# Hedgehog attention and a layer-normed MLP on one core: MLP groups of 512 tokens in place of 384, and every pair of batches worked off in units of two heads of one batch

## The chip, the cores and the metric

One core of a Trainium2 chip runs the whole program. The metric is the device time of one execution in microseconds (us): the kernel before takes 380.07 us, the median of 3 runs (379.72 to 380.33). "PE" is the matrix engine (TensorE), "PEld" its weight loads, "DVE" the vector engine, "ACT" the scalar engine, "POOL" GpSimd and "SP" the engine that issues nearly all transfers.

## What is computed

The inputs are q, k, v of shape 8 batches x 8 heads x 576 tokens x 64, a feature matrix 64 x 128, and the MLP's gain and two weight matrices (512 x 2048 and 2048 x 512).

```
def phi(x):
    proj = np.einsum('bhsd,df->bhsf', x, w_phi)
    proj = proj - np.max(np.abs(proj), axis=-1, keepdims=True)
    return np.concatenate([np.exp(proj), np.exp(-proj)], axis=-1)
q_p, k_p = (phi(q), phi(k))
kv = np.einsum('bhsf,bhsd->bhfd', k_p, v)
z = np.sum(k_p, axis=2)
num = np.einsum('bhsf,bhfd->bhsd', q_p, kv)
den = np.einsum('bhsf,bhf->bhs', q_p, z)[..., None] + 1e-06
...
# x: the 8 heads of num / den side by side, 8 x 576 x 512
xn = (x - mu) / np.sqrt(var + 1e-06) * g_ln
ch = np.maximum(xn @ w_ch1, 0.0) @ w_ch2
return (x + ch).astype(np.float32)
```

## The kernel before

**Tiles.** The 8 batches go in four pairs. The 576 tokens of a batch are 4 tiles of 128 and a rest of 64; the two rests of a pair make one "mixed" tile (MX = 8), so that a pair has NT = 9 tiles of 128 tokens, and the program 36.

**Attention** runs in 32 units, 8 to a pair, and a unit is two head-sequences. In pair 0 a unit is two heads of one batch: units 0 to 3 finish batch 0, units 4 to 7 batch 1. In pairs 1 to 3 a unit is one head of both batches, so that a batch is complete only when all 8 units of its pair are. PE turns or takes turned q and k (`qkT`), multiplies by the features (`pm` for k and q, `pt` for q the other way round, `n_bank` or `px` for the mixed tile), DVE takes the maxima (`m`, line 889), ACT the exponentials (`eb` line 903, `ea` line 971), POOL scales v (`vv`, line 915), PE multiplies features and values (`n_bank`, lines 997 and 1003) and then `num` (lines 1074 and 1080, in two parts), DVE joins and inverts (`numc`, `rden`, lines 1098 to 1110), and POOL writes the quotient into the bf16 `x` of the pair ("put", line 1118). In pair 0 half of the mixed rows lie on the wrong partitions: they go to `xs` and are moved by a transfer (line 1028) once per batch.

**The MLP** runs in 12 groups of RN = 384 tokens (three tiles), three groups to a pair. Of each tile the mean and variance are taken (`st`, `mv`), it is centred (`xc`) and turned, by PE in pair 0 (`xT_ps`) and by DMA transposes after. Then come 16 blocks of 4 matmuls 128x384 (`hT_ps`, line 1339), each evicted through a ReLU by ACT or DVE (lines 1349, 1347), and per tile 16 matmuls 128x512 (`ch_ps`, line 1406), whose result is scaled, joined with x and stored. Groups 0 to 2 are cut through the tiles in order: group 0 has tiles 0 to 2 of batch 0, so that it waits for units 0 to 3; groups 1 and 2 wait for all 8 units. In a later pair all three groups wait for the pair's last unit.

**Order of the work.** A planner written in the kernel (class `Order`) is run when the program is built. It is given every operation with an engine, a duration, what it reads and writes and which of the PSUM banks (A: 2 for `pm` and `pt`, N: 1, B: 3 for `hT_ps`, `ch_ps` and, in pair 0, `num`) it takes and frees. It picks for each engine the ready operation of the lowest rank; ranks are latest-start times plus offsets from the table `OFF`, by stage and by unit. The MLP's due times come from `DUE` and `BLOCK`. The result is one fixed instruction list for each engine. Where PE would idle before 75 us the planner puts in "fillers", small matmuls on zeros (line 1607), which keep PE occupied and compute nothing. PE waits in the order of its list: what stands behind a waiting instruction waits too.

Of the kernel before, what the change touches and what calls it, by code (L numbers as in the profile page):

```python
# [17 lines left out]
def bcast(ap: bass.AP, dim: int, n: int) -> bass.AP:  # L18
# [6 lines left out]
BLOCK = 17.68  # L25
# [8 lines left out]
FOLD = 0  # L34
# [4 lines left out]
        "load": 291.2, "trans": -8.3, "trans.copy": 32.9, "mixed": 7.1, "mixed.max": 32.9,  # L39
        "mixed.exp": 102.3, "mixed.fold": 0.0, "k": 28.8, "k.max": -2.5, "k.em": -28.4,  # L40
        "k.exp": -35.8, "en": 34.8, "vv": 1.8, "q": -0.7, "q.max": -15.1, "q.em": -14.1,
        "tails": -11.4, "tails.exp": -31.1, "kv": -2.9, "kv.copy": -20.8, "num0": -58.7,
        "num1": 49.3, "num.dve": -42.9, "g1": 0.0, "g2": 0.0, "g3": 0.0, "put": 7.3,
# [3 lines left out]
        "load": 291.2, "trans": -47.2, "trans.copy": 36.5, "mixed": 3.9, "mixed.max": 11.9,  # L47
        "mixed.exp": 12.0, "mixed.fold": 0.0, "k": 40.0, "k.max": -21.4, "k.em": 23.2,
        "k.exp": 42.8, "en": -19.5, "vv": 39.6, "q": -16.4, "q.max": 21.9, "q.em": -3.0,
        "tails": -100.2, "tails.exp": -42.9, "kv": 200.0, "kv.copy": -9.7, "num0": 87.9,  # L50
        "num1": 81.6, "num.dve": -5.2, "g1": 0.0, "g2": 0.0, "g3": 0.0, "put": -19.2, "ln": 5.4,
        "w1": -144.2, "w2": -136.8, "ln.c": -23.8, "ln.t": -23.8,
    },
    {
        "load": 291.2, "trans": 33.0, "trans.copy": 240.4, "mixed": -15.3, "mixed.max": -17.9,
        "mixed.exp": 83.6, "mixed.fold": 0.0, "k": 37.2, "k.max": -11.0, "k.em": -3.3,
        "k.exp": 18.4, "en": -32.8, "vv": 12.0, "q": 304.0, "q.max": -11.2, "q.em": -3.1,
        "tails": 103.2, "tails.exp": -35.5, "kv": 7.2, "kv.copy": 27.1, "num0": 39.1,
        "num1": 98.0, "num.dve": 2.1, "g1": 0.0, "g2": 0.0, "g3": 0.0, "put": -66.5,
        "ln": -23.8, "w1": -144.2, "w2": 26.3, "ln.c": -23.8, "ln.t": -23.8,  # L60
    },
    {
        "load": 291.2, "trans": 230.9, "trans.copy": 78.9, "mixed": 191.2, "mixed.max": -32.0,
        "mixed.exp": 33.8, "mixed.fold": 0.0, "k": -8.1, "k.max": 2.2, "k.em": -87.4,
        "k.exp": 26.7, "en": 11.2, "vv": -77.6, "q": -9.4, "q.max": 38.5, "q.em": -38.3,
        "tails": 16.8, "tails.exp": 26.2, "kv": 13.6, "kv.copy": 16.6, "num0": -1.3,
        "num1": 43.6, "num.dve": 21.7, "g1": 0.0, "g2": 0.0, "g3": 0.0, "put": 5.4, "ln": 14.4,
        "w1": -144.2, "w2": -136.8, "ln.c": 117.0, "ln.t": -36.8,
    },
    {  # L70
        "load": 14.8, "trans": -15.4, "trans.copy": -27.6, "mixed": 131.2, "mixed.max": -9.9,
        "mixed.exp": 10.9, "mixed.fold": 0.0, "k": -79.5, "k.max": -17.0, "k.em": 19.9,
        "k.exp": 31.1, "en": -13.2, "vv": -36.7, "q": 271.6, "q.max": 5.6, "q.em": 13.9,
        "tails": -412.8, "tails.exp": -3.4, "kv": 97.7, "kv.copy": 26.5, "num0": -27.8,
        "num1": -4.0, "num.dve": 68.7, "g1": 29.8, "g2": -16.9, "g3": -5.0, "put": -27.1,
# [3 lines left out]
        "load": 6.3, "trans": 29.0, "trans.copy": 24.9, "mixed": -2.7, "mixed.max": -13.2,  # L79
        "mixed.exp": -3.8, "mixed.fold": 0.0, "k": -79.5, "k.max": 30.5, "k.em": -14.6,  # L80
        "k.exp": -25.7, "en": -17.2, "vv": -13.4, "q": 271.6, "q.max": 28.1, "q.em": 39.7,
        "tails": -412.8, "tails.exp": 34.3, "kv": 2.4, "kv.copy": 35.9, "num0": 26.5,
        "num1": 69.2, "num.dve": 40.9, "g1": -233.9, "g2": -41.7, "g3": 25.5, "put": -6.4,
        "ln": 112.0, "w1": -341.2, "w2": -67.5, "ln.c": 107.2, "ln.t": 107.2,
    },
    {
        "load": 25.7, "trans": 38.5, "trans.copy": -37.8, "mixed": 31.6, "mixed.max": 60.6,
        "mixed.exp": 9.0, "mixed.fold": 0.0, "k": -79.5, "k.max": 11.5, "k.em": 44.1,
        "k.exp": 303.5, "en": 21.2, "vv": -17.8, "q": 271.6, "q.max": -32.9, "q.em": -6.4,
        "tails": -412.8, "tails.exp": -14.4, "kv": -2.0, "kv.copy": 123.1, "num0": 24.3,  # L90
        "num1": -4.7, "num.dve": 32.8, "g1": 92.8, "g2": 69.4, "g3": -5.0, "put": -14.8,
# [3 lines left out]
        "load": 6.3, "trans": 104.7, "trans.copy": -63.0, "mixed": -16.2, "mixed.max": -21.2,  # L95
        "mixed.exp": -28.3, "mixed.fold": 0.0, "k": -79.5, "k.max": -12.7, "k.em": -22.0,
        "k.exp": 14.6, "en": 103.8, "vv": 290.4, "q": 271.6, "q.max": -41.3, "q.em": 39.4,
        "tails": -412.8, "tails.exp": 4.2, "kv": -18.4, "kv.copy": -14.2, "num0": -20.5,
        "num1": 307.7, "num.dve": -20.9, "g1": -233.9, "g2": -41.7, "g3": 52.2, "put": 25.6,
        "ln": 131.6, "w1": -341.2, "w2": -67.5, "ln.c": 241.5, "ln.t": 47.3,  # L100
    },
    {
        "load": 276.1, "trans": 161.1, "trans.copy": 96.2, "mixed": -19.1, "mixed.max": -57.1,
        "mixed.exp": 54.1, "mixed.fold": 0.0, "k": -33.5, "k.max": 27.3, "k.em": 127.3,
        "k.exp": 30.4, "en": 12.5, "vv": 20.5, "q": -27.3, "q.max": 25.9, "q.em": 283.8,
        "tails": -210.6, "tails.exp": 11.0, "kv": 17.1, "kv.copy": -31.1, "num0": 152.9,
        "num1": 148.0, "num.dve": -174.3, "g1": 25.2, "g2": 33.5, "g3": -17.3, "put": -21.0,
        "ln": 196.2, "w1": -0.3, "w2": 28.2, "ln.c": 104.9, "ln.t": 37.2,
    },
    {  # L110
        "load": 4.0, "trans": 3.2, "trans.copy": 96.2, "mixed": -24.7, "mixed.max": -26.5,
        "mixed.exp": -33.8, "mixed.fold": 0.0, "k": -33.5, "k.max": 16.7, "k.em": -34.1,
        "k.exp": -3.4, "en": -54.3, "vv": 37.4, "q": -27.3, "q.max": 12.5, "q.em": 28.4,
        "tails": -210.6, "tails.exp": -22.6, "kv": 46.6, "kv.copy": -25.9, "num0": 16.8,
        "num1": 66.4, "num.dve": -83.9, "g1": 5.0, "g2": -21.1, "g3": -12.8, "put": -8.3,
        "ln": 20.8, "w1": 193.2, "w2": 28.2, "ln.c": 31.7, "ln.t": 4.8,
# [193 lines left out]
def kernel(  # L310
# [33 lines left out]
    RN = 384  # L344
    NR = ST // RN
    NM = RN // P
# [70 lines left out]
    for i in range(2):  # L417
# [5 lines left out]
    nident = consts.tile([P, P], BF16, name="nident")  # L423
    nc.vector.tensor_scalar(
        out=nident, in0=ident, scalar1=minus, scalar2=None, op0=ALU.mult
    )
# [4 lines left out]
    xs = consts.tile([P, 4, D], BF16, name="xs")  # L431

# [7 lines left out]
    ex_bufs = [consts.tile([P, 2, 2, P], BF16, name=f"ex{i}") for i in range(2)]  # L440
# [65 lines left out]
    def load_main(key, n, nu, rank, queue):  # L506
# [7 lines left out]
        if pair == 0:  # L514
# [5 lines left out]
            issue(  # L520
                queue, rank, dst.rearrange("p u (a f) -> p (u a) f", a=2), src,
                [(key + str(half), g % NBUF, u) for u in us for half in range(2)]
                + [("came", key, n)],
                262144 * nu,
            )
            return
# [212 lines left out]
    def a_mixed(u):  # L739
# [19 lines left out]
        def fold():  # L759
            subtract(u, u["px"][:, 2 * F : 3 * F], MX, u["mx"])  # L760

        def exps():
            ps = u["px"]
            for t, sc in ((0, 1.0), (1, -1.0)):
                if folded(n):
                    nc.scalar.activation(
                        u["EX"][:, t, :, :].rearrange("p s f -> p (s f)"), ps[:, F : 3 * F],
                        AF.Exp, scale=sc,
                    )
                    continue  # L770
# [195 lines left out]
    def a_tails(u):  # L966
# [680 lines left out]
```

## Time and profile before

| | |
|---|---|
| time | 380.07 us, median of 3 (379.72 to 380.33) |
| span of the profiled execution | 377.5 us, 2.57 us less than that median |
| PE busy | 363.6 us, 96% of the span, 3714 matmuls, 421 of them fillers |
| DVE, ACT, POOL busy | 250.5, 262.8, 203.4 us |
| DMA | 53.32 MB, mean 141 GB/s |

The profiled execution has no time of its own beside its span, so the 2.57 us (load, end of program) are taken as what lies around it. A matmul's recorded duration includes its way through the array; the pace of a run of equal matmuls is the time between starts. 128x384 goes at 0.1625 us and 128x512 at 0.2157 us. The profile of the program's second half shows PE alone at work with its evictions; the first 80 us show all engines busy and PE partly on fillers.

### The profile page before, as it was taken

The page shows a single profiled execution, that of the slowest core. Times are in us where ns is not written, and L with a number is a line of the kernel's source. Part 1 is how long each engine was busy: PE and PEld are TensorE (multiplying, and loading weights), DVE is VectorE, ACT ScalarE, POOL GpSimd, SP SyncE. Part 2 cuts the span into 40 slices and gives each one's busy share as a digit, 9 for nine tenths or more (in the row PEclk, how much of TensorE's full clock was granted, in tenths as well). Part 3 has the DMA queues.
Part 4 walks back from the last instruction along what each step waited for, and adds up shares of the span by engine and source line. Part 5 has one row for each costly group of instructions (what it writes and reads, how often), then busy time and mean ns, then how long its engine had stood idle before and what let it go on. Part 6 is the DMA issues. An engine that isn't in the chain of part 4 may idle for free.

```text
span 377.5 us, 9637 instructions
## 1 busy us (share of the span) xinstructions
PE 363.6 (96%) x3714; PEld 226.1 (60%) x3714; DVE 250.5 (66%) x548; ACT 262.8 (70%) x588; POOL 203.4 (54%) x347
## 2 busy tenths in 40 slices
PE   8998889799999999999999999999999999999995
PEld 8887766465656555665655555565565555555543
DVE  4788989997989879977877799587868200000001
ACT  2987978699697978896868778867846434444430
POOL 4399968659787754557857674635553001111121
PEclk9999999899999999999999999999999999999999
DMA  7999999899797867596826466500002520110012
GB/s 212 270 213 276 205 289 178 232 312 233 220 281 188 151 190 186 142 212 177 142 85 79 101 155 176 102 2 28 31 30 64 100 74 30 33 52 28 28 58 84
DMA packets 91086, 53.32 MB, mean 141 GB/s; under 512 B 57488, under 2 KB 86480, under 8 KB 91040
## 3 DMA queue, kind: packets, MB, share of 16 engines
q1 hardware_dynamic: 86000, 47.66, 52.1%
q0 software_dynamic: 4416, 4.49, 7.0%
q8 instruction: 29, 0.48, 0.5%
q10 hardware_dynamic: 624, 0.56, 0.5%
q14 instruction: 17, 0.14, 0.1%
HBM read 36.77 MB, written 9.44 MB: 122 GB/s over the span
## 4 chain that ended last, share of the span: by engine, by line
PE 79%; DVE 8%; DMA 6%; POOL 3%; ACT 1%; issue 1%; SPq 1%; ACTq 0%; DVEq 0%
PE hT_ps L1339 32%; PE ch_ps L1406 32%; DMA qk<-in_q_dram 4%; PE pm L827 3%; PE n_bank L1003 3%; DVE m L889 2%; PE num L1074 2%; DMA v<-in_v_dram 2%; PE pt L836 2%; PE n_bank L1074 1%; POOL vv L915 1%; PE n_bank L997 1%; PE ch_ps L1371 1%; DVE numc L1098 1%; DVE numc L1104 1%
## 5 line engine op out<-in xcount | busy, mean ns | idle before, releaser
L1339 PE MATMUL hT_ps<-xT,w 128*128 128x384 bf16 x768 | 153.2, 329 | 0.5 <-DVE numc L1098 0.3
L1406 PE MATMUL ch_ps<-w,hT 128*128 128x512 bf16 x560 | 148.1, 379 | 0.1
L1349 ACT ACTIVATE hT<-hT_ps 128x384 bf16<-128x384 f32 x125 | 61.6, 494 | 69.6 <-PE hT_ps L1339 69.2
L1339 PEld LDWEIGHTS <-w 128*128 128x128 bf16 x768 | 72.2, 99 | 56.7 <-issue 2.5
L889 DVE TENSOR_REDUCE m<-pm 128x8 f32<-128x1024 f32 x64 | 76.9, 1215 | 14.2 <-PE pm L827 12.2
L1406 PEld LDWEIGHTS <-hT 128*128 128x128 bf16 x560 | 51.1, 98 | 42.8 <-issue 1.2
L1118 POOL TENSOR_TENSOR x<-numc,rden 128x192 bf16<-128x192 f32 (+3 forms) x88 | 46.4, 541 | 47.3 <-DVE rden L1110 45.7
L903 ACT ACTIVATE eb<-pm 128x1024 bf16<-128x1024 f32 x64 | 64.7, 1038 | 7.6 <-DVE m L889 7.6
L971 ACT ACTIVATE ea<-pt 128x1024 bf16<-128x1024 f32 x64 | 63.7, 1039 | 5.1 <-PE pt L836 4.6
L1425 POOL TENSOR_TENSOR o<-o,x 128x512 f32<-128x512 f32 x20 | 23.1, 1156 | 80.3 <-ACT o L1419 80.3
L915 POOL TENSOR_TENSOR vv<-v,em 128x512 bf16<-128x512 f32 x32 | 34.0, 1064 | 34.4 <-issue 22.4
L1414 DVE SCALAR_TENSOR_TENSOR o<-ch_ps,rstd,x 128x512 f32<-128x512 f32 x15 | 11.2, 745 | 50.6 <-PE ch_ps L1406 50.6
L1347 DVE TENSOR_SCALAR hT<-hT_ps 128x384 bf16<-128x384 f32 x67 | 36.9, 553 | 11.6 <-PE hT_ps L1339 11.0
L915 POOL TENSOR_TENSOR vv<-v,en 128x512 bf16<-128x512 f32 x32 | 33.9, 1059 | 0.0
L1607 PE MATMUL n_bank<-wz 128*128 128x120 bf16 x421 | 30.7, 225 | 0.1
L1074 PEld LDWEIGHTS <-ea 128*128 128x128 bf16 x512 | 24.4, 97 | 8.1 <-issue 1.8
L1003 PE MATMUL n_bank<-vv,eb 128*128 128x65 bf16 x512 | 26.9, 194 | 0.0
L1607 PEld LDWEIGHTS <-wz 128*128 128x128 bf16 x421 | 26.0, 103 | 1.5 <-issue 0.5
L1003 PEld LDWEIGHTS <-eb 128*128 128x128 bf16 x512 | 22.3, 98 | 5.1 <-issue 1.5
L1261 DVE BATCH_NORM_STATS2 st<-x 128x6 f32<-128x512 bf16 (+1 forms) x44 | 24.6, 578 | 0.3 <-POOL x L1118 0.3
L1098 DVE TENSOR_TENSOR numc<-num,em 128x390 f32<-128x390 f32 (+1 forms) x40 | 20.6, 515 | 5.8 <-PE num L1074 5.5
L827 PE MATMUL pm<-wbk,qkT 64*128 64x128 bf16 x448 | 19.7, 217 | 2.8 <-ACT eb L903 2.8
(95 smaller groups left out, 456.8 us busy)
## 6 DMA issues: line engine op xcount, KB each, us to landing
qk<-in_k_dram SPq DMA_DIRECT2D x32, 256.0 KB, 4.9
qk<-in_q_dram SPq DMA_DIRECT2D x31, 256.0 KB, 5.5
v<-in_v_dram SPq DMA_DIRECT2D x31, 256.0 KB, 4.5
out_dram<-o SPq DMA_DIRECT2D x31, 256.0 KB, 2.5
w<-in_moe_w_ch_dram POOLq DMA_DIRECT2D x8, 512.0 KB, 11.5
out_dram<-o SPq DMA_DIRECT2D x10, 128.0 KB, 2.4
qx<-in_k_dram SPq DMA_DIRECT2D x16, 64.0 KB, 4.5
qx<-in_q_dram SPq DMA_DIRECT2D x14, 64.0 KB, 3.6
```

The lines of the kernel that those rows point to most:

```text
L889: nc.vector.reduce_max(out=m, in_=ps, axis=AX.X, apply_absolute_value=True)
L903: nc.scalar.activation(eb, ps, AF.Exp, scale=(1.0, -1.0)[t])
L915: nc.gpsimd.tensor_tensor(out=u["vv"][:, t, 0:MX, 0:D], in0=vb[:, hh, :].rearrange("p (c d) -> p c d", d=D), in1=bcast(e[:, 0:MX], 2, D), ...
L971: nc.scalar.activation(u["EA"][:, t, 0:1024], u["pt"], AF.Exp, scale=(1.0, -1.0)[t])
L1003: nc.tensor.matmul(ps[:, t, c // 4, :], EB[:, t, c, :], vv[:, t, c, :], start=False, stop=(t == 0 and c == MX - 1), skip_group_check=True,)
L1074: nc.tensor.matmul(ps[t][:, i, :], ea(u, t, c), KV[:, t, c // 4, :], start=True, stop=True,)
L1118: nc.gpsimd.tensor_tensor(out=dst, in0=st["numc"][ps_, i : i + n, 0:D], in1=bcast(st["rden"][ps_, i : i + n], 2, D), op=ALU.mult,)
L1339: nc.tensor.matmul(st["ps"], w1_sb[:, kc, jj * P : (jj + 1) * P], xT_bufs[(pair * NR + r) % XB][:, kc::KC, :], start=(kc == 0), stop=(kc = ...
L1347: nc.vector.tensor_relu(h_sb, st["ps"])
L1349: nc.scalar.activation(h_sb, st["ps"], AF.Relu)
L1406: nc.tensor.matmul(ch[t], hT[r, jj][:, rt * P : (rt + 1) * P], w2_sb[:, jj, :], start=(jj == 0), stop=(jj == JC - 1),)
L1607: nc.tensor.matmul(warm, wz, wz[:, 0:WN], start=False, stop=False, skip_group_check=True)
```

## The change

1. The MLP runs in nine groups of RN = 512 tokens (four tiles). Groups 2p and 2p+1 are the four full tiles of the two batches of pair p. The four mixed tiles of the program go to a tensor `xm` of their own and form one group, MIX, number 7; the second batch of pair 3 is group 8, LAST. 16 blocks of 4 matmuls 128x512 take the place of 128x384 ones.
2. All four pairs take pair 0's form: a unit is two heads of one batch (`BW = 4`). Group 2p then waits for the first four units of its pair, and group 2p+1 for the other four. Loads of pairs 1 to 3 become one transfer of 512 KB instead of two of 256 KB. Puts of these pairs go by head (3 tiles, 1 tile, 64 mixed rows), and the `xs` rows are moved once per batch in each pair: 8 moves instead of 2.
3. The `num` parts of pairs 1 to 3 take tiles (0,1,2,4,5,6) and (3,7,mixed) instead of 0 to 5 and 6 to 8; sizes are the same. `x` is tracked by tile, no longer by three.
4. The second product runs ahead of the first: a group's 64 `ch_ps` matmuls are offered within 10 of the next group's 16 blocks (`AHEAD_H`).
5. `hT` has 24 buffers of 512 instead of 34 of 384; unused code (`FOLD`, `nident`) goes. `BLOCK` and all of `OFF` have new numbers, so that every list is ordered anew.

```diff
-BLOCK = 17.68
+BLOCK = 23.57
...
-        "load": 291.2, "trans": -8.3, "trans.copy": 32.9, "mixed": 7.1, "mixed.max": 32.9,
+        "load": 291.2, "trans": -38.2, "trans.copy": 0.5, "mixed": 98.0, "mixed.max": 104.5,
...
-    RN = 384
-    NR = ST // RN
-    NM = RN // P
+    NM = 4
+    RN = NM * P
+    NR = MX // NM
+    LAST = NPAIR * NR
+    MIX = LAST - 1
+    HB = 24
+    AHEAD_H = 10
+    BW = 4
...
-        if pair == 0:
-            return i // 4, 2 * (i % 4) + half, 2
+        if pair < BW:
+            return 2 * pair + i // 4, 2 * (i % 4) + half, 2
...
-                out=u["x"][b * 64 : b * 64 + 64, MX, :].rearrange(
+                out=xm[b * 64 : b * 64 + 64, u["pair"], :].rearrange(
...
+    def token_tile(g, i):
+
+        pair, t = (i, MX) if g == MIX else (g // NR, g % NR * NM + i)
+        if g > MIX:
+            pair, t = NPAIR - 1, MX - NM + i
+        return pair, t, xm[:, i, :] if t == MX else pairs[pair]["x"][:, t, :]
...
+    def moe(g):
+
+
+        done = 0
+        for jj in range(JC):
+            if g <= LAST:
+                first(g, jj)
+            until = min(NM * JC, -(-(jj + 1) * NM * JC // AHEAD_H))
+            while g > 0 and done < until:
+                i, j0 = divmod(done, JC)
+                if g > LAST and i == NM - 1:
+                    break
+                n = min(until - done, JC - j0)
+                second(g - 1, i, j0, n)
+                done += n
...
-                half = i // 4 if i % 4 == 3 else None
...
+            if pair < BW:
+                groups = {3: (pair * NR,), 7: (pair * NR + 1,)}.get(i, ())
```

Counted over the whole lists, PE has 576 first-product matmuls of 128x512 where it had 768 of 128x384, 32 transposes of `xc` where it had 36, and 393 fillers after the first where it had 421; everything else on PE has the same count. POOL's puts rise from 96 instructions to 192. Of the 24 casts of q and k to bf16, DVE did 10, ACT 5 and POOL 9; now DVE does 3, ACT 14 and POOL 7.

**PE near unit 8**, the first unit of pair 1. `pm` and `pt` are its feature products, `n_bank<-wbk` the mixed tile's, `num` belongs to unit 7, `hT_ps` to group 0. Before:

```order
L1339 MATMUL hT_ps<-xT_139,w_134 128x384
...
L827 MATMUL pm<-wbk,qkT_142 128x128
...
L749 MATMUL n_bank<-wbk,qkT_142 128x256
...
L1074 MATMUL num<-KV,ea_127 128x65
...
L1080 MATMUL num<-KV,ea_127 128x65
...
L827 MATMUL pm<-wbk,qkT_143 128x128
...
L836 MATMUL pt<-qkT_143,wbk 128x512
...
L1339 MATMUL hT_ps<-xT_139,w_134 128x384
```

And in the changed kernel:

```order
L1019 MATMUL num<-KV,ea_127 128x65
...
L749 MATMUL n_bank<-wbk,qkT_141 128x256
...
L796 MATMUL pm<-wbk,qkT_141 128x128
...
L1246 MATMUL hT_ps<-xT_138,w_132 128x512
...
L749 MATMUL n_bank<-wbk,qkT_142 128x256
...
L1246 MATMUL hT_ps<-xT_138,w_132 128x512
...
L1013 MATMUL num<-KV,ea_127 128x65
...
L1246 MATMUL hT_ps<-xT_138,w_132 128x512
...
L796 MATMUL pm<-wbk,qkT_142 128x128
...
L805 MATMUL pt<-qkT_142,wbk 128x512
```

Between the two `pm` groups there stood both parts of `num`, one after the other, and no MLP matmul; now 16 `hT_ps` matmuls (8, 4 and 4) stand there, and the small part of `num` comes ahead of the first `pm` group.

**POOL in a unit of a later pair.** `vv<-...,em` and `vv<-...,en` scale v, the rows with `numc` are the puts. Before:

```order
L915 TENSOR_TENSOR vv<-v_101,em 128x8x64
...
L915 TENSOR_TENSOR vv<-v_101,en 128x8x64
...
L708 TENSOR_TENSOR b_1_147<-qk_100,one 128x1024
L1425 TENSOR_TENSOR o<-o,x 128x512
L1118 TENSOR_TENSOR x<-numc,rden 128x6x64
L1118 TENSOR_TENSOR x<-numc,rden 128x3x64
L915 TENSOR_TENSOR vv<-v_103,em 128x8x64
```

And in the changed kernel:

```order
L879 TENSOR_TENSOR vv<-v_101,em 128x8x64
...
L1057 TENSOR_TENSOR xm<-numc,rden 64x64
L879 TENSOR_TENSOR vv<-v_101,en 128x8x64
...
L1057 TENSOR_TENSOR xs<-numc,rden 64x64
L1057 TENSOR_TENSOR x<-numc,rden 128x64 x2
L1057 TENSOR_TENSOR x<-numc,rden 128x3x64 x2
L879 TENSOR_TENSOR vv<-v_101,em 128x8x64
```

Two puts per unit have become six, and some stand between or ahead of the scalings.

**SP at the end of attention** in the changed kernel (`xm<-xs` is the move of the mixed rows, `xT` are the transposes of groups 6, 8 and 7):

```order
L976 DMA xm<-xs 64x4x64
L1221 DMA out_dram<-o 128x512
L1161 DMA_TRANSPOSE xT_138<-xc_136 128x16x128
L1221 DMA out_dram<-o 128x512 x3
L976 DMA xm<-xs 64x4x64
L1161 DMA_TRANSPOSE xT_140<-xc_136 128x16x128
L1161 DMA_TRANSPOSE xT_139<-xc_137 128x16x128
L1221 DMA out_dram<-o 128x512 x4
```

Before, three transposes of 12 tiles for the last pair stood there, with no move ahead of them. On PE there stand behind the last `num` 16 `hT_ps` matmuls, 64 of `ch_ps` and 4 of `hT_ps` before the first that reads the MIX group's `xT_139`.

More of the change, by code (lines that the diff above doesn't have):

```diff
@@ L70 @@
-    {
[L71 to L75, printed above, removed]
+        "load": 291.2, "trans": 67.9, "trans.copy": 77.3, "mixed": 113.2, "mixed.max": 2.5,
@@ L110 @@
-    {
[L111 to L116, printed above, removed]
+        "load": 6.3, "trans": 1.6, "trans.copy": -2.9, "mixed": 203.3, "mixed.max": -49.1,
@@ L1050, in products @@
             KV = u["KV"]
[L1051 removed]
+            if part:
                 ps = n_bank if pair else ps_B.tile([P, 512], FP32, tag="B", name="num")
```

605 lines of the change are left out of this document (248 added, 357 removed), and 3 rows, old and new, of the table OFF.

## The prediction
> **What bounds the kernel now.** I read the page first, then the busy time by stage, then the chain of waits in order of time, and PE's own timeline where a stage had gaps. The page (part 2 has 40 slices of 9.4 us):
>
> ```profile
> span 377.5 us, 9637 instructions
> PE 363.6 (96%) x3714; PEld 226.1 (60%) x3714; DVE 250.5 (66%) x548; ACT 262.8 (70%) x588; POOL 203.4 (54%) x347
> PE   8998889799999999999999999999999999999995
> DVE  4788989997989879977877799587868200000001
> L1607 PE MATMUL n_bank<-wz 128*128 128x120 bf16 x421 | 30.7, 225 | 0.1
> ```
>
> PE is the bound, but its busy time holds 30.7 us of fillers, and the first eight slices have holes. Busy time by stage (columns: length, PE, PEld, DVE, ACT, POOL, granted clock, DMA share, GB/s):
>
> ```profile
> 40.00:60.00 20.00, 17.20 (x264) 13.12 (x262) 18.43 (x45) 17.66 (x40) 15.58 (x36) 1.00 1.23 249
> 60.00:80.00 20.00, 16.85 (x224) 11.43 (x223) 19.01 (x46) 15.84 (x34) 12.43 (x31) 0.91 0.90 224
> 80.00:100.00 20.00, 20.00 (x219) 11.81 (x218) 17.30 (x32) 17.71 (x40) 18.82 (x28) 1.00 1.01 238
> 100.00:180.00 80.00, 79.91 (x828) 47.31 (x825) 70.62 (x154) 66.78 (x158) 51.97 (x81) 1.00 0.81 197
> 180.00:260.00 80.00, 80.00 (x820) 46.77 (x818) 65.56 (x137) 62.79 (x147) 50.75 (x82) 1.00 0.47 96
> 300.00:377.50 77.50, 73.04 (x402) 39.12 (x400) 3.22 (x5) 29.59 (x58) 10.39 (x9) 1.00 0.16 50
> ```
>
> From 80 us on PE is never without work until the last product ends. What is gained or lost in total is therefore (a) PE work taken out, (b) PE time that is idle, slow or on fillers before 80 us, (c) any wait that the new lists make after 80 us. The chain of waits says the same and gives the paces (first line its shares, then start, length, what):
>
> ```profile
> PE 79%; DVE 8%; DMA 6%; POOL 3%; ACT 1%; issue 1%; SPq 1%; ACTq 0%; DVEq 0%
> 71.04 4.19 PE hT_ps L1339 x16
> 159.01 3.25 PE hT_ps L1339 x20
> 361.99 7.55 PE ch_ps L1406 x35
> ```
>
> At 159 us a 128x384 matmul takes 3.25/20 = 0.1625 us, at 362 us a 128x512 one 7.55/35 = 0.2157 us. At 71 us sixteen 128x384 took 4.19 us where 2.60 were due: 1.6 us lost, in the one stage whose granted clock is below 1 (0.91).
>
> What precedes those slow sixteen is the largest hole of PE, in its timeline (start, length, instruction, in brackets the idle time before it and who ended it), with ACT's and DVE's below:
>
> ```profile
> 63.55 1.21 PE L1607 MATMUL n_bank<-wz 128*128 128x120 bf16 x20
> 64.60 0.22 PE L997 MATMUL n_bank<-vv,eb 128*128 128x130 bf16 x1
> 65.66 0.62 PE L827 MATMUL pm<-wbk,qkT 64*128 64x128 bf16 x16
> 66.39 0.60 PE L1074 MATMUL num<-KV,ea 128*128 128x65 bf16 x14
> 66.95 0.22 PE L1080 MATMUL num<-KV,ea 128*128 128x65 bf16 x2
> 69.94 0.40 PE L827 MATMUL pm<-wbk,qkT 64*128 64x128 bf16 x8 [2.76 <-ACT eb L903]
> ```
>
> ```profile
> 66.64 1.18 DVE L889 TENSOR_REDUCE m<-pm 128x8 f32<-128x1024 f32 x1
> 69.67 0.55 DVE L1104 TENSOR_TENSOR numc<-numc,num 128x390 f32<-128x390 f32 x1
> ```
>
> ```profile
> 67.85 1.02 ACT L903 ACTIVATE eb<-pm 128x1024 bf16<-128x1024 f32 x1 [1.59 <-DVE m L889]
> 68.87 1.02 ACT L903 ACTIVATE eb<-pm 128x1024 bf16<-128x1024 f32 x1
> ```
>
> The sixteen `pm` matmuls take both A banks. The next `pm` waits until DVE has its maxima (66.64) and ACT both exponentials (to 69.89). No MLP block fills the hole, because `num` of unit 7, both parts, holds all three B banks, and DVE releases the first two only with the `numc` sum that starts at 69.67.
>
> **The change, part by part.** The sum is made against the span of 377.5 us; the median of the runs lies 2.57 us above it, and I add that at the end.
>
> *PE work.* 768 x 0.1625 = 124.8 us becomes 576 x 0.2157 = 124.2: -0.6 (the same columns in 192 fewer instructions). Four transposes of `xc` fewer: -0.2 at most. All other matmuls keep their counts and shapes.
>
> *Fillers.* The lists hold 28 fewer. The twenty at 63.55 go to 64.60, 0.0525 us each, so 28 take 1.5 us. By position, 39 fewer stand behind the first `hT_ps` (40 before, one now) and 11 more ahead of it. The cover in the later place is real work: group 0 now offers 64 matmuls of 0.2157 = 13.8 us and as much again in second products where it offered 10.4 twice, at the same point of attention. I take -1.5; the bounds are 0 (PE waits there without a filler) and -2.0 (all 39 gained, the 11 hidden).
>
> *The hole at 67 us.* The new list puts 8 + 4 + 4 `hT_ps` of 0.2157 us, 3.5 us, and the mixed tile of the next unit between the two `pm` groups, and the small part of `num` ahead of the first, so that the B banks are not all held at once. The `pm` group then asks for its bank about 4 us after the first one, and the chain it waits for is 1.18 + 2 x 1.02 = 3.2 us plus hand-overs (65.66 to 69.94 in the trace). Whole gain: 2.76 idle and 1.6 of slow clock, -4.4. Against it: DVE is busy 19.01 of 20 us in that stage, so its part of the wait can turn up elsewhere. I take -2.8, nearer to the full gain than to 0, because MLP blocks no longer depend on the place where DVE is late; bounds 0 and -4.4. The Trainium skill, page "TensorE: Matmul & The Clock Gate", section "Part 1: The HAM clock gate", says that the array falls to half clock after an idle window of about 3.4 us and needs a busy one of that length to come back. The trace agrees in kind: slow matmuls right behind a 2.76 us gap. By that rule the change is risky where it drops fillers: a gap that stays brings the 1.6 us back with it; if it closes they go together.
>
> *The start of the MLP.* Group 0 needs a fourth tile's statistics, centring and turn. In the list 36 fillers (1.9 us) stand ahead of the first transposes, and the first `hT_ps` comes behind 1.3 us more attention than before. I take +0.5, about one tile's centring (rows below); bounds -0.5 and +2.
>
> *The other engines.* Rows for them:
>
> ```profile
> L1118 POOL TENSOR_TENSOR x<-numc,rden 128x384 bf16<-128x384 f32 x24 | 20.3, 849 | 16.0 <-DVE rden L1110 15.1 <-DVE mv L1275 0.8
> L1118 POOL TENSOR_TENSOR x<-numc,rden 128x192 bf16<-128x192 f32 x40 | 20.0, 507 | 30.7 <-DVE rden L1110 30.6
> L1118 POOL TENSOR_TENSOR x<-numc,rden 128x64 bf16<-128x64 f32 x16 | 4.4, 291 | 0.2
> L1349 ACT ACTIVATE hT<-hT_ps 128x384 bf16<-128x384 f32 x125 | 61.6, 494 | 69.6 <-PE hT_ps L1339 69.2
> L1347 DVE TENSOR_SCALAR hT<-hT_ps 128x384 bf16<-128x384 f32 x67 | 36.9, 553 | 11.6 <-PE hT_ps L1339 11.0
> L706 ACT CAST b<-qk 128x1024 bf16<-128x1024 f32 x5 | 5.2, 1043 | 0.0
> L704 DVE CAST b<-qk 128x1024 bf16<-128x1024 f32 x10 | 8.4, 845 | 0.1
> L1284 ACT ACTIVATE xc<-x,mv 128x512 bf16<-128x512 bf16 x17 | 12.0, 731 | 0.1
> PE n_bank L997 <- POOL vv L924: 0.9, 2, 0.6
> ```
>
> Puts of a later unit cost POOL 849 + 507 = 1356 ns; now 2 x 507 + 4 x 291 = 2178. That is 0.82 us a unit, 19.7 us for 24 units. POOL was busy 18.82 + 51.97 + 50.75 = 121.5 of the 180 us from 80 to 260, 68%; with 19.7 more 78%. ACT takes nine more casts (9.4 us) and fewer but longer ReLUs; the 384-wide one takes 494 ns and the 1024-wide cast 1043, so 128 columns more cost some 0.11 us, 93 x 0.604 = 56.2 against 61.6. ACT rises by about 4 us and DVE falls by about 6 (seven casts). No engine comes to PE's load, and PE waited 0.9 us in all for POOL's `vv`. I take +0.5, half as much again as that wait; the bounds are 0 and +4 (a fifth of POOL's extra time on PE's path).
>
> *Transfers.* The same bytes for q, k, v in fewer, longer transfers, six small moves more and seven long transposes for nine short ones. From 100 us the DMA share is at most 0.81, and before 60 us (1.23) pair 0's loads keep size and form: 0.
>
> *The last groups.* The MIX group waits for the last unit by a longer way:
>
> ```profile
> x<-xs SPq DMA_DIRECT2D x2, 32.0 KB, 5.2
> xT<-xc SPq DMA_TRANSPOSE x9, 3.8
> L1261 DVE BATCH_NORM_STATS2 st<-x 128x6 f32<-128x512 bf16 x28 | 18.3, 672 | 0.0
> L1098 DVE TENSOR_TENSOR numc<-n_bank,em 128x195 f32<-128x195 f32 x24 | 8.5, 355 | 2.9 <-POOL x L1118 1.3 <-PE n_bank L1080 1.0 <-ACT b L706 0.3
> ```
>
> Two `numc` passes and the inverse 0.9, four small puts 1.2, the move 5.2, statistics 0.7, centring 0.7, a transpose of 16 tiles for 12 3.8 x 16/12 = 5.1: 13.8 us, with hand-overs some 15. Behind the last `num` PE's list has 16 + 64 + 4 matmuls of 0.2157 = 18.1 us of cover. Hidden: 0. Without that cover each us over 18.1 is a us of the total; bound +2.
>
> Sum: -0.6 - 0.2 - 1.5 - 2.8 + 0.5 + 0.5 = -4.1, a span of 373.4 and, with 2.57, **376.0 us**. The end (products over at 373.05, last result and store) stays.
>
> **The rivals.**
>
> *A. The start is set by DVE, ACT and DMA, and PE's gaps only move.* For it: DVE 18.43 and 19.01 of 20 us, DMA share 1.23. Against: MLP work that fills gaps needs little of DVE, and more of it is on offer. Then the hole, and its slow clock, stay in some form and half of the filler time comes back as waiting: -0.8 - 0.75 + 0.5 = -1.05, 379.0 us.
>
> *B. POOL becomes late, slower than before.* Place: `kv` of every unit in pairs 1 to 3. Puts stand ahead of or between the two `vv` scalings, PE's list waits at `kv`, and with it the MLP blocks behind. Price: up to 0.82 us a unit, 19.7 in all. It decides from the point where a fifth of it, 4.1 us, lands on PE. For it: POOL at 18.82 of 20 us from 80 to 100. Against: 68% on the whole, and `vv` now waits for maxima more often than for POOL. Half of the 19.7 would give 380.1 - 4.6 + 9.85 = 385.3; a typical case 382.5.
>
> *C. The gain is larger:* hole and slow clock go whole and nothing turns up elsewhere: -0.6 - 0.2 - 1.5 - 4.4 = -6.7, 373.4 us.
>
> *D. The change does not do what it says:* groups start no earlier, since a batch's rows arrive late. Against: in PE's list the first group of pair 1 begins with 14 units' `kv` done, before with 17. Then 379.5, with the last groups' way as the late one.
>
> **How the numbers follow.** Forecast 376.0 with chance 0.48 (its own range 374.3 to 378.0, from taking the hole at -4.4 to -0.8); A 0.22, B 0.12, C 0.13, D 0.05. The range that leaves out no more than 2 in 10: below it a third of C, above it most of B and a little of A and D: 373.0 to 380.2. About 0.2% (0.8 us) is what this measurement tells from no change. Faster than 379.3: all of forecast and C, 0.7 of A, 0.3 of D: 0.78. Within 0.2%: the rest of A and D and a little of B: 0.10. Slower: 0.12.
>
> **What would show it.** In the profile after: PE's window 60 to 80 us busy 19 or more of 20 and its granted clock 1.0 (the hole); the wait of `pm` for `eb` under 1 us; 128x512 at 0.2157 throughout; PE's waits on POOL `vv` under 2 us in all; no PE wait before the MIX group's first block; first `hT_ps` at 52 to 54 us. Wrong if PE waits stand behind 80 us, if the hole appears at another instruction, or if the first `hT_ps` is later than 55 us.

## The result, and the profile after

The changed kernel takes 375.25 us (median of four runs, 374.74 to 376.04), the kernel before beside it 380.13: a ratio of 0.987, interval 0.984 to 0.990. Forecast were 376.0 us. The profiled execution has a span of 373.7 us (forecast 373.4) and a time of its own of 375.46, so that 1.8 us lie around its span, not the 2.57 the prediction added. By 1.8, the profile before (span 377.5) stands for an execution of 379.3 us, 0.8 under its median: the two profiles show 3.8 of the 4.9 us that lie between the medians.

The page of the changed kernel, its parts 1, 2 and 5:

```profile
span 373.7 us, 9165 instructions
PE 358.2 (96%) x3490; PEld 204.4 (55%) x3490; DVE 244.2 (65%) x517; ACT 271.0 (73%) x564; POOL 216.3 (58%) x441
...
PE   8968898998999999999999999999999999999995
...
L1512 PE MATMUL n_bank<-wz 128*128 128x120 bf16 x393 | 28.4, 222 | 0.6 <-ACT KV L961 0.5
```

Busy time by stage (length, PE, PEld, DVE, ACT, POOL, granted clock, DMA share, GB/s):

```profile
20.00:40.00 20.00, 15.07 (x274) 12.83 (x271) 15.66 (x37) 13.59 (x35) 17.04 (x37) 1.00 1.04 217
...
60.00:80.00 20.00, 18.49 (x179) 9.71 (x178) 18.36 (x40) 15.82 (x32) 14.54 (x30) 1.00 1.00 227
80.00:100.00 20.00, 18.50 (x178) 10.00 (x176) 15.96 (x34) 15.22 (x35) 13.77 (x25) 1.00 0.99 242
100.00:180.00 80.00, 79.83 (x778) 42.60 (x777) 64.08 (x128) 67.96 (x144) 51.30 (x110) 1.00 0.74 187
```

From 60 to 80 us PE is busy 18.49 us at full clock; before it was 16.85 at 0.91. From 80 to 100 us it is busy 18.50 us, before it was 20.00. PE's waits and its timeline at four places show what came and what went (start, length, instruction, in brackets the idle time before it):

```profile
PE qkT_ps L633 <- DMA qk<-in_q_dram: 3.6, 3, 2.7
PE pt L805 <- DVE numc L1043: 1.5, 1, 1.5
PE n_bank L945 <- POOL vv L888: 1.1, 2, 0.6
```

```profile
25.68 0.40 PE L633 MATMUL qkT_ps<-ident,qk 128*128 128x128 bf16 x4 [2.67 <-DMA qk<-in_q_dram]
...
55.31 1.03 PE L1246 MATMUL hT_ps<-xT,w 128*128 128x512 bf16 x4
...
67.61 0.62 PE L796 MATMUL pm<-wbk,qkT 64*128 64x128 bf16 x16
68.17 1.90 PE L1246 MATMUL hT_ps<-xT,w 128*128 128x512 bf16 x8
...
70.07 1.03 PE L1246 MATMUL hT_ps<-xT,w 128*128 128x512 bf16 x4
70.93 0.53 PE L1013 MATMUL num<-KV,ea 128*128 128x65 bf16 x12
71.88 1.02 PE L1246 MATMUL hT_ps<-xT,w 128*128 128x512 bf16 x4 [0.41 <-DVE hT L1254]
72.83 0.40 PE L796 MATMUL pm<-wbk,qkT 64*128 64x128 bf16 x8
...
93.38 0.39 PE L805 MATMUL pt<-qkT,wbk 64*128 64x512 bf16 x2 [1.50 <-DVE numc L1043]
```

At 72.83 the second `pm` finds its bank free: the hole of 2.76 us is gone. New are 2.67 us of waiting for q at 25 us and 1.50 us at 93 us.

The end of the chain of waits shows PE with nothing but MLP work behind the last `num`, whole runs at 0.216 us a matmul (3.45/16, 13.81/64, 14.68/68):

```profile
297.34 3.45 PE hT_ps L1246 x16
300.80 13.81 PE ch_ps L1312 x64
314.61 14.68 PE hT_ps L1246 x68
...
366.41 3.51 PE ch_ps L1278 x32
369.92 0.03 issue
```

**Where the time went.** The span fell by 3.8 us. It splits at two points that both traces pass. The first `hT_ps` starts at 55.31 us, before at 52.21: +3.10, of which the list moves 1.3 ahead of it (attention work, which is saved behind it), so 1.8 are a loss. From there to the last product's end it takes 369.92 - 55.31 = 314.61 us, before 373.05 - 52.21 = 320.84: -6.23. The last eviction and store take 3.78 instead of 4.45: -0.67. So the gain is made between the first `hT_ps` and the end; a part of it is given back ahead of the first `hT_ps` and at 93 us.

PE's busy time in the two stretches says what the 6.23 us are (before, then after; the columns are those of the stages above):

```profile
52.21:373.05 320.84, 317.14 (x2928) 184.57 (x2924) 209.28 (x449) 223.61 (x500) 164.61 (x260) 0.99 0.53 127
```

```profile
55.31:369.92 314.61, 311.29 (x2660) 162.10 (x2656) 201.21 (x412) 230.36 (x471) 173.73 (x349) 1.00 0.52 129
```

PE was idle 320.84 - 317.14 = 3.70 us before and is 314.61 - 311.29 = 3.32 us now. The hole's 2.76 us are gone, but about as much idle time stands elsewhere: 1.5 us at 93 us, 1.1 for `vv`, 0.4 for `hT`. What fell is busy time, by 5.85 us: 39 fillers of 0.0525 us less (2.0), the slow clock behind the hole (1.6), the 1.3 of attention moved ahead and 0.8 of PE work make 5.7 of it.

### The profile page after: what moved, and what is told of

It reads as the page before. It is cut to its first block, busy times and chain, and to the rows that moved or that the text cites. A ratio compares the mean times of both kernels' runs of the same rounds, so it can differ in the third digit from the quotient of the medians.

```text
span 373.7 us, 9165 instructions
## 1 busy us (share of the span) xinstructions
PE 358.2 (96%) x3490; PEld 204.4 (55%) x3490; DVE 244.2 (65%) x517; ACT 271.0 (73%) x564; POOL 216.3 (58%) x441
## 4 chain that ended last, share of the span: by engine, by line
PE 75%; DMA 14%; DVE 7%; POOL 1%; issue 1%; SPq 0%; DVEq 0%; POOLq 0%
PE ch_ps L1312 29%; PE hT_ps L1246 29%; DMA qk<-in_q_dram 8%; DMA qkT<-b 4%; PE pm L796 3%; PE n_bank L951 3%; PE num L1013 3%; DVE m L853 2%; PE pt L805 2%; DMA qx<-in_k_dram 2%; PE n_bank L1512 1%; PE ch_ps L1278 1%; PE n_bank L945 1%; DVE numc L1037 1%; DVE hT L1254 1%
## 5 line engine op out<-in xcount | busy, mean ns | idle before, releaser
L1246 PE MATMUL hT_ps<-xT,w 128*128 128x512 bf16 x576 | 137.3, 379 | 0.5 <-DVE hT L1254 0.4
L1312 PE MATMUL ch_ps<-w,hT 128*128 128x512 bf16 x560 | 132.5, 379 | 0.0
L1246 PEld LDWEIGHTS <-w 128*128 128x128 bf16 x576 | 52.1, 98 | 56.2 <-issue 2.8
L1256 ACT ACTIVATE hT<-hT_ps 128x512 bf16<-128x512 f32 x93 | 55.6, 598 | 30.8 <-PE hT_ps L1246 29.4
L1057 POOL TENSOR_TENSOR x<-numc,rden 128x64 bf16<-128x64 f32 (+1 forms) x128 | 48.4, 401 | 20.8 <-DVE rden L1049 19.2
L1254 DVE TENSOR_SCALAR hT<-hT_ps 128x512 bf16<-128x512 f32 x51 | 35.0, 687 | 12.1 <-PE hT_ps L1246 11.7
L1325 ACT ACTIVATE o<-ch_ps,rstd 128x512 f32<-128x512 f32 x22 | 15.1, 687 | 28.2 <-PE ch_ps L1312 28.2
L1512 PE MATMUL n_bank<-wz 128*128 128x120 bf16 x393 | 28.4, 222 | 0.6 <-ACT KV L961 0.5
L1512 PEld LDWEIGHTS <-wz 128*128 128x128 bf16 x393 | 23.9, 101 | 2.1 <-issue 1.2
L1329 POOL TENSOR_TENSOR o<-o,xm 128x512 f32<-128x512 f32 x4 | 4.6, 1153 | 31.7 <-ACT o L1325 31.7
```

Of the source, the lines that this page charges most:

```text
L1057: nc.gpsimd.tensor_tensor(out=dst, in0=st["numc"][ps_, i : i + n, 0:D], in1=bcast(st["rden"][ps_, i : i + n], 2, D), op=ALU.mult,)
L1246: nc.tensor.matmul(st["ps"], w1_sb[:, kc, jj * P : (jj + 1) * P], xT_bufs[g % XB][:, kc::KC, :], start=(kc == 0), stop=(kc == KC - 1),)
L1254: nc.vector.tensor_relu(h_sb, st["ps"])
L1256: nc.scalar.activation(h_sb, st["ps"], AF.Relu)
L1312: nc.tensor.matmul(ch[g, i], hT[g, jj][:, i * P : (i + 1) * P], w2_sb[:, jj, :], start=(jj == 0), stop=(jj == JC - 1),)
L1512: nc.tensor.matmul(warm, wz, wz[:, 0:WN], start=False, stop=False, skip_group_check=True)
```

## The experiments

Two statements were in question: the prediction's, that the hole at 67 us and the fillers were PE time on the path, and rival A's, that DVE, ACT and DMA set the start and PE's gaps only move. Experiments e1 to e4 ran on one chip, e5 to e8 on another, e9 to e12 on a third; each ratio is to the kernel before on the same chip.

### e5: the changed kernel again

> The changed kernel itself once more, beside the others, so that they can be compared with it on one chip. Theory and rivals alike: 375.2 us, a ratio to the kernel before of 0.987 (within 0.984 to 0.990). If it comes out near 378, the three experiments on the changed kernel so far have to be read again, since their ratios were compared with the 0.987 of another chip.

376.04 us (374.3 to 377.7), ratio 0.9879, interval 0.984 to 0.992. So 0.988 is what the others are held against; its interval alone is 1.5 us wide to either side, and single executions of the changed kernel spread over 3.4 us. Its profile (span 372.5 us) differs from the first where the start is concerned. Its stages, its first `hT_ps`, and the end of its last product in the chain of waits:

```profile
20.00:40.00 20.00, 15.66 (x246) 13.86 (x245) 15.21 (x33) 12.71 (x28) 16.43 (x36) 0.83 1.16 237
60.00:80.00 20.00, 19.29 (x181) 10.10 (x182) 19.28 (x41) 16.84 (x33) 14.89 (x30) 1.00 0.96 231
80.00:100.00 20.00, 19.89 (x190) 10.98 (x191) 17.41 (x39) 16.98 (x39) 15.11 (x27) 1.00 1.01 238
```

```profile
57.42 1.03 PE L1246 MATMUL hT_ps<-xT,w 128*128 128x512 bf16 x4
```

```profile
368.77 0.02 issue
```

The first `hT_ps` starts 2.1 us later than in the other profile, and yet the span is 1.2 us shorter: PE is busy 19.29 and 19.89 us in the next stages, and the wait at 93 us isn't there. From its first `hT_ps` to the end of its last product it takes 368.77 - 57.42 = 311.35 us, 3.3 less than the other profile (314.61) with the same lists. So the start of the MLP alone doesn't set the end: here a later start was made up by shorter waits behind it.

### e1: the hole in the kernel before, closed by hand

```diff
+        to = at(("num", 7, 0), ("PE",))
...
+        for i in later[0:MOVE]:
+            key = next(k for k in done[i].keys if k[0] == "hT_ps")
+            ahead += [i, at(key, ("ACT", "DVE"))]
...
+        done[to:to] = ops
```

(MOVE is 3: three blocks of `hT_ps` and their evictions.)

> The kernel before, with three hT_ps blocks (and their evictions) of group 0 moved ahead of unit 7's num on every list, so that they stand in the hole at 67 us; nothing else is moved. Theory P (PE time lost before 80 us is lost in full): the 2.76 us wait and the 1.6 us of slow clock go, the time falls by 2.5 to 4.4 us to some 376 to 377.5. Rival A (the start is set by DVE, ACT and DMA; PE's gaps only move): the gap turns up at the next pm or num, the time falls by less than 1 us.

380.96 us, ratio 1.0028, interval 1.000 to 1.005: nothing gained. PE and DVE of this kernel (the line numbers are shifted):

```profile
66.82 2.11 PE L1353 MATMUL hT_ps<-xT,w 128*128 128x384 bf16 x12
...
72.13 0.40 PE L841 MATMUL pm<-wbk,qkT 64*128 64x128 bf16 x8 [2.20 <-ACT eb L917]
```

```profile
68.32 0.56 DVE L1361 TENSOR_SCALAR hT<-hT_ps 128x384 bf16<-128x384 f32 x1 [1.17 <-PE hT_ps L1353]
68.80 1.21 DVE L903 TENSOR_REDUCE m<-pm 128x8 f32<-128x1024 f32 x1
```

The blocks ran where they were put, but one eviction went with them, onto DVE's list ahead of the maxima. DVE stood 1.17 us for `hT_ps` and spent 0.56 on the eviction, 1.73 us together. The first maximum began at 68.80 instead of 66.64 (2.16 later), and the second `pm` at 72.13 instead of 69.94 (2.19 later). The other 0.43 is a shift of the whole profile, whose first `hT_ps` starts at 52.64 instead of 52.21 us. The gap moved by what DVE was held up. So the run shows that the place of an eviction on DVE's list matters as much as the block's on PE's; it does not show that the hole was worthless.

### e6: the hole put back into the changed kernel

```diff
+        for i in pe[at - 6 : at + 3]:
+            if has(i, "hT_ps"):
+                key = next(k for k in done[i].keys if k[0] == "hT_ps")
+                ahead += [i, next(j for j, o in enumerate(done) if j > i and key in o.keys)]
...
+        to = next(i for i in pe[at:] if has(i, "pt"))
```

> The changed kernel with the four blocks (16 hT_ps of 0.2157 us) that stand between the two groups of pm around 68 to 72 us put behind the second pm and pt, with their evictions; nothing else moves. Theory of the prediction (the hole is worth 2.8 to 4.4 us and the blocks close it): PE waits at the second pm for about 2.5 us again, its clock in that stage falls to about 0.9, and the time is 2.8 to 4.4 us more than the changed kernel's. Rival (as the move of three blocks in the kernel before, which gained nothing, suggests: DVE and ACT set that stretch, and the wait only changes place): within 1 us of the changed kernel.

378.88 us, ratio 0.9940, interval 0.992 to 0.997: 2.8 us more than the changed kernel beside it by medians, 2.3 by the ratios. The interval just touches that of e5 (0.9915 against 0.9918) and lies clear of the first measurement's (0.990). Its stage and PE's timeline:

```profile
60.00:80.00 20.00, 16.02 (x145) 8.37 (x144) 13.75 (x29) 13.39 (x28) 13.08 (x26) 0.91 1.08 242
```

```profile
64.98 3.62 PE L1262 MATMUL hT_ps<-xT,w 128*128 128x512 bf16 x16
...
70.53 0.27 PE L765 MATMUL n_bank<-wbk,qkT 128*128 128x256 bf16 x1 [0.96 <-ACT ea L782]
...
72.51 0.40 PE L812 MATMUL pm<-wbk,qkT 64*128 64x128 bf16 x8 [1.29 <-DVE m L869]
73.28 0.39 PE L821 MATMUL pt<-qkT,wbk 64*128 64x512 bf16 x2 [0.38 <-ACT eb L883]
73.61 5.31 PE L1262 MATMUL hT_ps<-xT,w 128*128 128x512 bf16 x16
```

The waits are back, 0.96 + 1.29 + 0.38 = 2.6 us, and behind them sixteen matmuls take 5.31 us where the same sixteen took 3.62 eight microseconds before: 1.7 us of slow clock. Of 4.3 us lost here, 2.3 to 2.8 reach the end. The theory of the prediction holds, at or a little below the low end of what was expected (2.8); the rival's "within 1 us" is the less likely, though two intervals that touch don't shut it out alone.

### e2: PE work added in the same stretch

```diff
-            for kc in range(KC):
+            for kc in [*range(KC)] * (2 if g == 0 and 10 <= jj < 15 else 1):
```

Five blocks of group 0 are computed twice, the second time over the first.

> The changed kernel with five hT_ps blocks of group 0 (blocks 10 to 14) multiplied twice into the same bank: 20 more matmuls of 0.2157 us, 4.3 us of PE work between 68 and 77 us. Theory P: the time rises by about 4.3 us, to 379.5. Rival A: PE has slack there that other engines make, the time rises by less than 1.5 us.

378.56 us, ratio 0.9954, interval 0.994 to 0.997. Against 0.988 that is +2.9 us for 20 x 0.2157 = 4.3 us of work, more than the rival's 1.5 and less than the theory's 4.3. About two thirds of the PE time added at 68 to 77 us reaches the end, which agrees with e6 (2.3 to 2.8 of 4.3). A part is absorbed: PE time there is on the path, but not all of it.

### e8 and e9: the fillers left out

In e8 all 393 of the changed kernel, in e9 only the 40 behind the first `hT_ps` of the kernel before:

```diff
-    sched.filler = ("PE", WARM, mm(1, WN), fill)
+    sched.filler = ("PE", WARM, mm(1, WN), lambda: None)
```

```diff
+        start = next(i for i, o in enumerate(done) if ("hT_ps", 0, 0, 0) in o.keys)
+        done = [o for i, o in enumerate(done) if i < start or o.number >= 0]
```

> The changed kernel without its 393 fillers in the lists; everything else keeps its order. Theory of the prediction (a filler only covers time in which PE would wait anyhow; those ahead of the first hT_ps cost nothing): within 1 us if the clock stays, but the gap of 2.76 us in the kernel before was followed by matmuls at 0.26 us in place of 0.1625. Rival (the fillers hold the clock): PE's useful work of the first 60 us, some 30 us, runs partly at a lower clock, granted clock below 0.9 in those stages, and the time is 3 to 10 us longer. Third: faster by up to 2 us, because a filler that is on the way delays work that is ready.

> The kernel before without the 40 fillers that stand behind its first hT_ps (20 of them at 63.55 to 64.60 us); everything else keeps its order. Theory of the prediction (its filler term, -1.5, with 28 to 39 fillers of 0.0525 us that delay real work): 1.5 to 2.1 us faster than the kernel before, a ratio near 0.995. Rival (as with all 393 left out of the changed kernel: they stand where PE waits anyhow): the same within 0.5 us, a wait of n_bank or pm appearing in their place. Third: slower, as the stage of the hole then loses its clock earlier.

e8: 375.38 us, ratio 0.9840, interval 0.981 to 0.988; no slower than the changed kernel's 0.9879, whose interval it overlaps. e9: 381.73 us, ratio 1.0034, interval 1.001 to 1.006; slower, if anything. The stages of e8, then PE's waits of e9:

```profile
0.00:20.00 20.00, 13.44 (x116) 10.32 (x118) 11.57 (x34) 10.37 (x20) 8.63 (x19) 0.74 0.99 256
20.00:40.00 20.00, 12.96 (x200) 10.21 (x202) 18.48 (x42) 17.19 (x43) 19.70 (x42) 0.95 1.04 207
40.00:60.00 20.00, 14.55 (x178) 10.64 (x178) 15.26 (x37) 15.50 (x38) 17.94 (x41) 0.63 1.17 241
60.00:80.00 20.00, 19.39 (x182) 10.11 (x183) 19.39 (x43) 17.09 (x33) 13.63 (x29) 1.00 1.04 230
```

```profile
PE pm L829 <- ACT eb L905: 2.9, 1, 2.9
PE n_bank L999 <- POOL vv L926: 2.6, 4, 0.8
```

In e9 PE's waits for `vv` rise from 0.9 to 2.6 us in four places and the hole stays (2.9 instead of 2.76): the fillers stood where PE had to wait, as the rival said. In e8 the granted clock falls to 0.74 and 0.63 in two stages, so the rival's mechanism (the fillers hold the clock) happens; its price does not. PE is busy 13.0 to 14.6 of 20 us in the three stages before 60 us, so it has time to spare there.

### e7 and e10: two transposes ahead of four loads

SP's timeline of the changed kernel, and the view of its transposes of q and k from 75 to 95 us with those who waited for them:

```profile
81.58 0.51 SPq L483 DMA_DIRECT2D qk<-in_q_dram  x1
82.19 9.31 SPq L727 DMA_TRANSPOSE qkT<-b  x3
```

```profile
  DVE b L699: 2.5, 1
...
DMA to landing us min/median/max: 3.8/5.9/9.2
```

Four loads of 512 KB were issued from 80.07 to 81.58 us, directly ahead. In the kernel before, four transfers of 256 KB stand ahead of its three transposes, and the last line of the same view reads:

```profile
DMA to landing us min/median/max: 4.3/5.0/6.4
```

DVE's 2.5 us are at 91.97 us, ahead of the `numc` for which PE's `pt` waits at 93.38. e7 moves two transposes ahead of the loads, e10 leaves out the fillers as well:

```diff
+        p, to = turns[3], sp[turns[4]]
+        loads = sp[p - 4 : p]
...
+        done[to + 1 : to + 1] = ops
```

> The changed kernel with two transposes of q and k (units 11 and 12) ahead of the four 512 KB loads that precede them on SP at 80.07 to 81.58 us; nothing else moves. Theory: the 9.23 us that the first of them took to land at 82.19 is the time of the 2 MB of loads ahead of it, and it is what makes DVE wait 2.55 us at 91.97 and PE 1.50 us at 93.38 and, through it, the steps around. Then landing falls to about 4 us, PE's waits between 80 and 100 us fall from 1.5 to under 0.3, and the time falls by 1 to 2 us. Rival (the wait is set by the order of DVE's list, or the loads, now later, are themselves waited for): within 0.5 us, or slower.

> The changed kernel with both edits at once: the two transposes ahead of the four loads, and no fillers. If they act in different places (around 91 us, and before 57 us), their effects add: 375.2 - 2.3 - 0.7 = 372 to 373 us, a ratio of 0.979 to 0.982. If either was only a shift of the same wait, it is no better than the transposes alone, 0.982 to 0.984.

e7: 373.75 us (372.85 to 375.85), ratio 0.9822, interval 0.979 to 0.986; e10: 373.48 us, 0.9818, interval 0.979 to 0.985. SP's timeline and the view of its transposes in e7:

```profile
81.91 2.79 SPq L735 DMA_TRANSPOSE qkT<-b  x2
84.75 0.59 SPq L491 DMA_DIRECT2D qk<-in_k_dram  x1
```

```profile
DMA to landing us min/median/max: 3.2/3.4/9.5
```

The two land in about 3.4 us (the third, still behind the loads, in 9.5), PE does not wait for `numc` any more, and the median is 2.3 us lower than the changed kernel's beside it. But the intervals of 0.9822 and 0.9879 overlap, and the profiles of e5, e2 and e4 have the late landing (10.1, 9.4 and 10.0 us) without the wait at 93 us. In e6, where two of the four loads go 3.4 us ahead of the other two, the transposes behind them land in 5.6 us at most. That the loads delay the transposes is shown; that the 2.3 us come from it is not. e10 is level with e7: its ratio lies where its two forecasts meet (0.979 to 0.982 if the effects add, 0.982 to 0.984 if not), so it does not tell them apart, and a second gain clear of noise is not there. e7 and e10 are the fastest kernels of the study by their medians.

### e3: a quarter of w1 later

```diff
+        def late():
+            if n == 2:
+                held.append(emit)
+                return
```

> The changed kernel with the load of the third quarter of the first weights issued on POOL beside the fourth, behind those of the second weights, instead of beside the first two; no other instruction is moved. Theory L (that load took the way of q and k of units 4 to 6 and made PE's waits of 2.7 and 0.8 us at 22 to 33 us, and with them the late first hT_ps at 55.3 us): the waits fall under 1 us together, the first hT_ps comes at 53 us or earlier, the time falls by 1 to 2.5 us to about 373.5. Rival S (the start is paced by POOL's and DVE's work for units 0 to 3): the first hT_ps stays at 55 us and the time within 0.5 us of 375.3.

378.42 us, ratio 0.9952, interval 0.992 to 0.998: some 2.8 us slower than 0.988, not faster. In its profile PE's waits for q fall from 3.6 to 2.0 us, those for POOL's `vv` rise from 1.1 to 3.3, and the first `hT_ps` stays at 55.48 us where theory L had 53. Neither forecast came true: the start stayed, as rival S said, but the time did not. The late start is not explained by that transfer alone, and what explains it stays open.

### e4: POOL's puts done twice

```diff
+                if pair and part:
+                    put(u["x"][:, t0 : t0 + ht, cols], full, half * ht, ht)
```

> The changed kernel with both one-tile puts of every unit of pairs 1 to 3 done twice (the same values): 48 x 0.29 = 14 us more on POOL, nothing told to the planner. Theory P: POOL has room at 58%, the time rises by less than 1 us. Rival B (POOL's puts stand ahead of vv and PE waits): at least a fifth of the 14 us lands on PE, 3 us or more.

377.25 us, ratio 0.9931, interval 0.990 to 0.996. POOL's busy time rises from 216.3 to 230.4 us and the median by 2.0 us over 0.988, with intervals that overlap. That is one seventh of the 14 us, under the fifth from which rival B decides, but above the 1 us of the theory: it lies between the two forecasts and decides for neither.

### e11 and e12: parts of the change alone

```diff
-    BW = 4
+    BW = 1
```

> The changed kernel with BW = 1: groups of 512 tokens, the MIX group and the new offsets, but pairs 1 to 3 in the old units (one head of both batches), so that both groups of a pair wait for its eighth unit; the planner orders every list anew and puts in 502 fillers. Theory (the earlier groups of pairs 1 to 3 matter little, since PE is never without work from 100 us on; the gain is in the first 80 us, in pair 0): if the plan before 80 us stays good, within 2 us of the changed kernel. Rival (the units bring the gain, or the offsets fit only them): slower than the changed kernel by 4 us or more, with PE waits behind 100 us or a later first hT_ps.

> The changed kernel with the offsets of the kernel before, so groups and units without the new order of the lists; the planner puts in 598 fillers, all ahead of the first hT_ps. Theory (what closes the hole and feeds PE is the order of the lists; the groups alone take out 0.6 us of PE work): slower than the kernel before, 385 us or more, because the first hT_ps comes later by the time of some 200 fillers (10 us) less what other work moves into that stretch. Rival (groups and units bring the gain by themselves): within 3 us of the changed kernel.

e11: 414.61 us, ratio 1.0905 (1.088 to 1.094). My expectation, within 2 us of the changed kernel if the plan before 80 us stayed good, was far off; the rival's, 4 us or more slower with PE waits behind 100 us, came true. PE starves in the middle:

```profile
100.00:180.00 80.00, 65.94 (x654) 37.23 (x658) 59.07 (x123) 59.70 (x134) 57.05 (x92) 0.87 0.70 174
```

e12, the same groups and units with the offsets of before: 387.06 us, ratio 1.0183 (1.015 to 1.021), its first `hT_ps` at 64.16 us: as expected, 385 us or more. Both are slower than the kernel before, so neither part brings the gain with lists made for something else; neither run says what groups or units would bring with lists made for them, so that share stays open.

## Why the prediction was right, and where it was not

**PE work, -0.6 and -0.2.** Held: 128x512 goes at 0.216 us in the long runs of the chain.

**The hole, -2.8.** Held in mechanism, and in size as far as the noise lets one say. The wait of `pm` for `eb` is gone and the granted clock of the stage is 1.0; putting the gap back costs 2.3 to 2.8 us. The reason given for taking -2.8 and not -4.4 was that part of the wait would turn up elsewhere. It does: in the first profile PE's idle time behind the first `hT_ps` falls by 0.4 us only, though the slow clock (1.6) is gone whole. e2 and e6 put it in numbers: of 4.3 us lost at this place 2.3 to 2.9 reach the end, some 55 to 65%, each figure good to about 1.7 us by the intervals.

**Fillers, -1.5.** This step failed as it was priced. Fillers cost nothing where they stood: e9 takes out the 40 late ones and gains nothing, since waits come in their place, and e8 takes out all 393 and the time stays. They cannot be counted at 0.0525 us each; what can bring time is other work put into the wait beneath them. The account of PE's busy time shows that this can have happened (39 fillers, 2.0 us, are gone behind the first `hT_ps`, and PE's idle time did not grow), but no run isolates it from the hole.

**Start of the MLP, +0.5.** Mis-sized: 1.8 us lost. Ahead of it PE waits 3.6 us for q, 2.67 of it at 25 us, where the prediction had put the transfers at 0; that these waits make the late start is not shown, since e3 shortens them to 2.0 us and the start stays. The first `hT_ps` came at 55.31 us, beyond the 55 that I had named as a sign of error. e5 shows why that sign was badly chosen: it starts at 57.42 and ends sooner.

**Transfers, 0.** Wrong in two places: the q loads of pair 0 came late, though their size and form are the same, and the 512 KB loads of later pairs delay the transposes behind them from 6.4 to 9.2 us, with 1.5 us of PE waiting at 93 us in the first profile and none in e5's. I had argued from the DMA share, a mean over a stage, for the time before 60 and behind 100 us, and not from what stands in one queue ahead of a transfer that is waited for. By e7's median some 2.3 us lie there, by its interval it may be none.

**Other engines, +0.5.** Held: PE waited 1.1 us for `vv`, before 0.9. POOL rose by 12.9 us, less than the 19.7 set down for its puts alone, and ACT by 8.2, twice the forecast. Rival B, slower than before, did not come; e4 adds that 14 us more on POOL cost about 2 us.

**Last groups, 0.** Held: PE goes from `ch_ps` to `hT_ps` of the MIX group at 314.61 us without a gap.

So the sum came out (-3.8 against -4.1 by the spans, -4.9 by the medians) with one term that held about its size (the hole), one that no run bears out as priced (fillers), two losses that were too small (start, transfers), and a tail that got shorter by 0.67 us where it was to stay. The "wrong if" signs came (a wait of 1.5 us behind 80 us, at another instruction, and a first `hT_ps` behind 55 us), and the window from 60 to 80 us was busy 18.49 us in one profile, 19.29 in the other, where 19 had been named: that the total came out so close is in part luck, since terms of opposite sign offset each other. Rival A was half right: the late start and the untouched time of e8 show that PE is not the bound before 57 us, but from 60 us on its gaps count by about a half or more.

## What to carry to other kernels

Before pricing a gap or a filler, ask whether the engine is the bound at that place: here 28 us of fillers cost nothing, nearly all of them before 57 us, and PE time lost at 70 us cost some 60% of itself. The cheap test is to leave the fillers out or to add work there. When work is moved into a gap, look where its evictions land on the next engine's list, since in e1 one eviction ahead of the maxima held DVE 1.73 us and nothing was gained. Larger transfers with the same bytes are a change of their own: what is queued right behind them can land later, here in up to 9.2 us instead of 6.4.

## What was not expected of the hardware

Without fillers PE's granted clock was 0.74 from 0 to 20 us and 0.63 from 40 to 60 us, and the time did not rise (0.984 against 0.988). The Trainium skill, page "TensorE: Matmul & The Clock Gate", section "Part 1: The HAM clock gate", says that half clock is the default and that sustained work of about 3.4 us lifts it. The rows of e8 agree in part: the clock fell in stages in which PE had lost its fillers, but not in the order of its busy time, since the stage with the least, 12.96 us, kept 0.95. The low clock cost no time here, which fits PE having time to spare in these stages.

The gaps of e6 were 0.96, 1.29 and 0.38 us with small matmuls between them, and the sixteen matmuls behind them ran at 5.31/16 = 0.33 us. Three stretches of e6 show where the clock fell (columns as above, the granted clock behind POOL):

```profile
67.60:71.02 3.42, 2.46 (x44) 1.73 (x43) 3.37 (x9) 1.57 (x6) 1.89 (x1) 1.00 0.99 184
71.02:74.43 3.41, 1.75 (x21) 0.92 (x18) 2.90 (x8) 2.81 (x8) 2.90 (x8) 1.00 0.81 276
74.43:77.85 3.42, 3.42 (x9) 1.18 (x8) 0.00 (x0) 1.98 (x4) 2.14 (x5) 0.50 1.11 350
```

The first stretch, with PE busy 2.46 of 3.42 us, kept the full clock behind it; behind the second, with 1.75 of 3.41 us, the clock was half for 3.42 us. By that section of the Trainium skill an idle window is about 3.4 us long; here a stretch that was only partly idle was enough, each gap being shorter than half of that.
